# Batch 1's stage A moved onto quarter arrays: casting half loads of x, an earlier read of u, products from slot 8

## The chip, the cores and the metric

The kernel runs on one core of one Trainium2 chip. The metric is the device time of that core in microseconds (us), from the first instruction to the last. The time before is the median of three runs.

## The reference

```python
def _attn_ref(x, filt_r, filt_i):                 # x: 8 batches x 3008 rows x 256 channels
    X = np.fft.rfft(x, axis=1)
    Y = X * (filt_r + 1j * filt_i)[None, :, :]
    return np.fft.irfft(Y, n=x.shape[1], axis=1)

def _moe_ref(x, w_in, w_out):                     # 24064 rows, 256 -> 2048 -> 256
    h = np.maximum(x @ w_in, 0.0)
    return h * h @ w_out
```

The output is the second function of the first one's result: a filter by Fourier transform along the rows of each batch, then a feed-forward layer with a squared ReLU over all rows.

## The kernel before

A batch has 3008 = 64 x 47 rows, and its transform is done by matmuls in stages. Stage A takes x (64 blocks of 47) to **u**; u goes to DRAM (dU) and comes back in another order (`read_u`, tile ut). Stage B (`unit_b`) takes ut to frequencies and multiplies with the filter (DVE, the product), after which a DMA adds the two halves of the product. Stage P (`unit_p`) takes products to **z**; z goes to DRAM (dZ) and back (`read_z`, tile zt). Stage Y (`unit_y`) turns zt into yt, the input of the feed-forward layer.

The feed-forward layer runs in 47 groups of 512 rows, eight **slots** a group. Slot s does the first matmuls of group s // 8 (`ffn_g1`: four matmuls of 512 columns, then a ReLU on ACT into h, which DVE squares), and a share of the second matmuls of the group before (`ffn_g2` for the first group, `products` of seven half-size products with sums on DVE for the others). The stages of the later batches are put between these by a plan. Batch 0 goes through its stages ahead of slot 0, in a prologue.

Batch 1 is the special case that the change is about. Before, it loads x in float32 through SyncE's queue, casts it on three engines, and does stage A with full-array matmuls of 96 output rows, three quarters of it in the prologue and one quarter in slots 8 and 9:

```python
def load_wide(b, k):                              # 1 MB each, b = 0 and 1, k = 0..2
    ...
    nc.sync.dma_start(out=t, in_=(v0[:, 0:8, :], v1, v0[:, 8:16, :])[k])

def write_u(b, c):
    u = us.pop((b, c))
    if b == 1:
        nc.sync.dma_start(out=dU[b].rearrange("(m q) d -> q m d", q=96)[:, 8 * c:8 * c + 8, :], in_=u)
        return
    v = dU[b].rearrange("(m q) d -> q m d", q=48)
    for j in range(2):
        m = 16 * c + 8 * j
        nc.sync.dma_start(out=v[:, m:m + 8, :], in_=u[64 * j:64 * j + 48])

def unit_a1(b, a):                                # batch 1, one sixteenth; L354, L356
    ...
    nc.tensor.matmul(ps[0:96, :], s1[:, c // 2, :], xw16[(b, 2 * (c % 2))][:, m, :], start=True, stop=False)
    nc.tensor.matmul(ps[0:96, :], s1[0:120, 2 + c, :], xw16[(b, 1)][0:120, m, :], start=False, stop=True)
    ...                                           # copied to u by ACT (a even) or DVE (a odd)

def unit_a(b, c):                                 # batches 2 to 7, one quarter; L378
    u = us[(b, c)] = p_u.tile([112, 8, D], F16, tag="u", ...)
    ph = psH(...); ps = [psF(...) for h in range(2)]
    for i in range(2):
        for j in range(2):
            m = slice(4 * j + 2 * i, 4 * j + 2 * i + 2)
            for h in range(2):
                p = slice(64 * h, 64 * h + N2)
                o = ps[h] if i == 0 else ph[:, h, :]
                nc.tensor.matmul(o[64 * j:64 * j + 64, :], sSA[p], x16s[(b, c)][p, m, :], start=True, stop=True)
    ...                                           # three copies to u, then write_u

def chunk_a(b, c):                                # batch 1, one quarter, in the prologue; L400, L402
    ...                                           # 8 matmuls of 512 columns, copied to u by ACT or DVE

def load_x(b, k):                                 # half of a quarter of x, cast by the DMA
    ...
    nc.gpsimd.dma_start(out=t[64 * h + p0:64 * h + p1], in_=v[p0:p1, 8 * c:8 * c + 8, :])

def read_u(b):
    ut = p_ut.tile([128, NC, D], F16, tag="ut", name=f"ut_{b}")
    v = dU[b].rearrange("(p s) d -> p s d", s=NC)
    for s0, s1 in ((0, 8), (8, 24)):
        nc.sync.dma_start(out=ut[:, s0:s1, :], in_=v[:, s0:s1, :])
    uts[b] = ut
```

The end of the prologue and the plan's part for batch 1 (f is 0 there, and 40 for batch 2):

```python
cast_win()                                        # w_in to float16, GpSimd
for k in range(2):
    cast_wide(1, k, nc.gpsimd, nc.gpsimd)
...                                               # batch 0: stages B and P; each sixth of z is written to dZ
cast_wide(1, 2, nc.vector, nc.scalar)
read_z(0, 0)
load_wout(0)                                      # 1 MB
read_z(0, 1)
load_wout(1)                                      # 1 MB
for c in (0, 2, 1):
    chunk_a(1, c)
for c in (0, 2, 1):
    write_u(1, c)
for n in range(4):
    unit_y(0, n)
prologue[0] = False
read_z(0, 2)
...
    if b == 1:
        ...                                       # unit_y(0, n) for n = 4 to 15 in slots 4 to 23.5
        for a in range(12, 16):
            fixed.append((2 + a / 2, unit_a1, b, a))
        moves.append((10.5, read_u, b))
        d = 7
    ...
    for p in range(12):
        r = 14 + 15 * p / 11 if b == 1 else 6 + 28 * p / 11 if b == 2 else -2 + 36 * p / 11
        units.append((f + r, unit_b, b, p))
        if b == 1 and 2 <= p < 10:
            moves.append((f + r, load_x, 2, p - 2))
        units.append((f + r + (4.5 if b == 1 else 7 - 2.5 * p / 11), unit_p, b, p))
    for c in range(4):
        moves.append((f + (40 + d / 14, 43, 48, 54)[c] - d, read_z, b, c))
```

Engines run their instructions in program order, and so does SyncE's DMA queue: a transfer that waits holds up those behind it. [...]

Of the kernel before, what the change touches and what calls it, by code (L numbers as in the profile page):

```python
# [26 lines left out]
def _build_consts():  # L27
# [72 lines left out]
    f16 = lambda a, p: np.ascontiguousarray(a.reshape(p, -1).astype(np.float16))  # L100
    C0 = np.zeros((128, 1472))
    C0[:, 0:576] = S0.reshape(128, 6, 2, 2, NC).transpose(0, 1, 4, 2, 3).reshape(128, 576)
    C0[:, 576:704] = np.eye(128)
    C0[:, 704:1280] = S0.reshape(128, 576)
    for h in range(2):
        C0[64 * h:64 * h + N2, 1280:1328] = SA[:, h, h].reshape(N2, 48)
    C0[:, 1376:1470] = SY.reshape(128, 94)
    return f16(C0, 128), f16(PF, 128), f16(SB, 128), f16(SP, 128)


@with_exitstack
def kernel(
# [85 lines left out]

    sC0 = p_t.tile([128, 1280], F16, tag="t", name="sC0")
    sC1 = const.tile([128, 192], F16, name="sC1")  # L200
    nc.scalar.dma_start(out=sC0[:, 0:704], in_=dC0.ap()[:, 0:704])
    s0 = sC0[:, 0:576].rearrange("p (w q) -> p w q", q=96)
    s1 = sC0[:, 704:1280].rearrange("p (w q) -> p w q", q=96)
    sSA = sC1[:, 0:64]
    sSY = sC1[0:112, 96:190]
    ident = sC0[:, 576:704]
# [3 lines left out]

    def load_wide(b, k):

        v0 = xrows[b * S:b * S + 2048, :].rearrange("(p m) d -> p m d", m=16)
        v1 = xrows[b * S + 2048:b * S + 3072, :].rearrange("(p m) d -> p m d", m=8)
        pool, tag = (p_x32, "x32") if k < 2 else (p_y, "yt") if b else (p_h2, "h2")
        t = pool.tile([128, 8, D], F32, tag=tag, name=f"xw_{b}_{k}")
        nc.sync.dma_start(out=t, in_=(v0[:, 0:8, :], v1, v0[:, 8:16, :])[k])
        xw32[(b, k)] = t

    def cast(eng, out, in_):  # L220
        (eng.copy if eng is nc.scalar else eng.tensor_copy)(out=out, in_=in_)

    def cast_wide(b, k, *engs):
        t = p_x16.tile([128, 8, D], F16, tag="x16", name=f"xw16_{b}_{k}")
        for i in range(2):
            m = slice(4 * i, 4 * i + 4)
            cast(engs[i], t[:, m, :], xw32[(b, k)][:, m, :])
        xw16[(b, k)] = t

    for k in range(3):  # L230
        load_wide(0, k)

# [12 lines left out]
    load_f(1)  # L245
    nc.sync.dma_start(out=sC0[:, 704:1280], in_=dC0.ap()[:, 704:1280])
    nc.sync.dma_start(out=sC1, in_=dC0.ap()[:, 1280:1472])
    nyq = p_out.tile([128, 2, D], F32, tag="ost", name="nyq")
# [87 lines left out]
    def write_u(b, c):  # L336
        u = us.pop((b, c))
        if b == 1:
            nc.sync.dma_start(
                out=dU[b].rearrange("(m q) d -> q m d", q=96)[:, 8 * c:8 * c + 8, :], in_=u)  # L340
            return
        v = dU[b].rearrange("(m q) d -> q m d", q=48)
        for j in range(2):
            m = 16 * c + 8 * j
            nc.sync.dma_start(out=v[:, m:m + 8, :], in_=u[64 * j:64 * j + 48])

    def unit_a1(b, a):

        c, i = divmod(a, 4)
        if i == 0:  # L350
            us[(b, c)] = p_u.tile([96, 8, D], F16, tag="u", name=f"u_{b}_{c}")
        ps = psF(f"psA_{b}_{a}")
        m = slice(2 * i, 2 * i + 2)
        nc.tensor.matmul(ps[0:96, :], s1[:, c // 2, :], xw16[(b, 2 * (c % 2))][:, m, :],  # L354
                         start=True, stop=False)
        nc.tensor.matmul(ps[0:96, :], s1[0:120, 2 + c, :], xw16[(b, 1)][0:120, m, :],  # L356
                         start=False, stop=True)
        o = us[(b, c)][:, 2 * i:2 * i + 2, :]
        pv = ps[0:96, :].rearrange("p (a d) -> p a d", d=D)
        if a % 2 == 0:  # L360
            nc.scalar.copy(out=o, in_=pv)
        else:
            nc.vector.tensor_copy(out=o, in_=pv)
        if i == 3:
            write_u(b, c)

    def unit_a(b, c):

        u = us[(b, c)] = p_u.tile([112, 8, D], F16, tag="u", name=f"u_{b}_{c}")
        ph = psH(f"psA_{b}_{c}")  # L370
        ps = [psF(f"psA_{b}_{c}_{h}") for h in range(2)]
        for i in range(2):
            for j in range(2):
                m = slice(4 * j + 2 * i, 4 * j + 2 * i + 2)
# [3 lines that stand above are left out]
                    nc.tensor.matmul(o[64 * j:64 * j + 64, :], sSA[p], x16s[(b, c)][p, m, :],  # L378
                                     start=True, stop=True)
        for h in range(2):  # L380
            o = u[:, h:h + 3:2, :]
            pv = ps[h][0:112, :].rearrange("p (e d) -> p e d", d=D)
            if h == 0:
                nc.scalar.copy(out=o, in_=pv)
            else:
                nc.vector.tensor_copy(out=o, in_=pv)
        nc.scalar.copy(out=u[:, 4:8, :].rearrange("p (e h) d -> p h e d", h=2),
                       in_=ph[0:112].rearrange("p h (e d) -> p h e d", d=D))
        write_u(b, c)

    def chunk_a(b, c):

        u = p_u.tile([96, 8, D], F16, tag="u", name=f"u_{b}_{c}")
        us[(b, c)] = u
        for k in range(2):
            banks, groups = bank_pair(f"psA_{b}_{c}_{k}")
            for i in range(2):
                m = slice(4 * k + 2 * i, 4 * k + 2 * i + 2)
                o = banks[i][0:96]
                nc.tensor.matmul(o, s1[:, c // 2, :], xw16[(b, 2 * (c % 2))][:, m, :],  # L400
                                 start=True, stop=False)
                nc.tensor.matmul(o, s1[0:120, 2 + c, :], xw16[(b, 1)][0:120, m, :],  # L402
                                 start=False, stop=True)
            eng = pair_engine()
            for t, i in groups:
                n = t.shape[1]
                o = u[:, 4 * k + 2 * i:4 * k + 2 * i + 2 * n, :]
                pv = t[0:96].rearrange("p t (a d) -> p (t a) d", d=D)
                if eng is nc.scalar:
                    eng.copy(out=o, in_=pv)  # L410
                else:
                    eng.tensor_copy(out=o, in_=pv)

    def chunk_a0(c):

        for k in range(2):
            banks, groups = bank_pair(f"psA_0_{c}_{k}")
            for dt in range(2):
                for i in range(4):
                    m = 4 * k + i  # L420
                    o = banks[dt][:, 96 * i:96 * i + 96]
                    d = slice(128 * dt, 128 * dt + 128)
                    nc.tensor.matmul(o, xw16[(0, 2 * (c % 2))][:, m, d], s0[:, c // 2, :],
                                     start=True, stop=False)
                    nc.tensor.matmul(o, xw16[(0, 1)][0:120, m, d], s0[0:120, 2 + c, :],
                                     start=False, stop=True)
# [288 lines left out]
    def fft_plan():  # L715

        fixed, units, moves = [], [], []
        for b in range(1, B):
            f = (b * S // TG) * SLOTS - (48 if b > 1 else 40)
            d = 0  # L720
            if b == 1:
# [4 lines left out]
                for k in range(4):  # L726
                    moves.append(((4.5, 5.5, 7.5, 7.5)[k], cast_wout, k, nc.vector))
                for a in range(12, 16):
                    fixed.append((2 + a / 2, unit_a1, b, a))
                moves.append((10.5, read_u, b))  # L730
                d = 7
# [9 lines left out]
            for p in range(12):  # L741
                r = 14 + 15 * p / 11 if b == 1 else 6 + 28 * p / 11 if b == 2 else -2 + 36 * p / 11
                units.append((f + r, unit_b, b, p))
                if b == 1 and 2 <= p < 10:
                    moves.append((f + r, load_x, 2, p - 2))
                units.append((f + r + (4.5 if b == 1 else 7 - 2.5 * p / 11), unit_p, b, p))
# [38 lines left out]
    for k in range(3):  # L785
        cast_wide(0, k, nc.vector, nc.gpsimd if k == 2 else nc.vector)

# [8 lines left out]
    load_win()  # L796
    for k in range(3):
        load_wide(1, k)
    for c in (0, 2, 1, 3):
# [20 lines left out]
    for k in range(6):  # L820
# [3 lines left out]
        nc.gpsimd.tensor_copy(out=sSPx[-1][0:64, o, :], in_=sSP[64:128, c, :])  # L824
        nc.gpsimd.tensor_copy(out=sSPx[-1][64:128, o, :], in_=sSP[0:64, c, :])
    cast_win()
    for k in range(2):
        cast_wide(1, k, nc.gpsimd, nc.gpsimd)
    for k in range(7):
# [7 lines left out]
        if k < 4:  # L837
            place_f(0, k + 2, nc.scalar)
    cast_wide(1, 2, nc.vector, nc.scalar)
    read_z(0, 0)  # L840
    load_wout(0)
    read_z(0, 1)
    load_wout(1)
    for c in (0, 2, 1):
        chunk_a(1, c)
    for c in (0, 2, 1):
        write_u(1, c)
    for n in range(4):
# [55 lines left out]
```

## Time and profile before

| what | value |
|---|---|
| time, median of 3 (lowest to highest) | 760.14 us (759.89 to 760.58) |
| span of the profiled run | 758.9 us |
| TensorE busy in the records | 743.8 us, 98% |
| DVE, ACT, GpSimd busy | 653.1, 565.9, 191.7 us |
| prologue: first matmul of slot 0 | at 49.06 us |
| first matmul of slot 8 | at 58.24 us |
| casts of batch 1's x | GpSimd 34.94 to 38.9 us, DVE at 40.16, ACT at 41.84 |
| stage A of batch 1 in the prologue (24 matmuls) | 40.73 to 45.97 us |
| stage A of batch 1 in slots 8 and 9 (8 matmuls) | 59.61 to 63.96 us |
| `read_u` of batch 1, issue | at 68.17 us |
| first `unit_b` of batch 1, slot 14 | at 72.45 us |
| a GpSimd x load (batch 2 on), from issue to landing | 5.0 us median on the page |

The records of a matmul overlap[...]: one of 512 columns shows 380 ns, and the next can start 216 ns later. So a short wait is better seen between the starts of matmuls than in the idle time. A row of the stage table gives the stretch, its length, the busy time and number of instructions of each engine, then the granted clock, the share of the DMA engines and their rate. In the timeline of SyncE's queue the first number is the start and the second the time that the issues took with the waits among them.

### The profile page before, as it was taken

How to read it: one execution, taken by the hardware profiler on the slowest of the kernel's cores; microseconds unless marked ns; L12 is line 12 of the kernel's file. 1: busy time of each engine (PE TensorE's matmuls, PEld its weight loads, DVE VectorE, ACT ScalarE, POOL GpSimd, SP SyncE). 2: the span in 40 equal slices, each digit the busy share in tenths (PEclk: the TensorE clock that was granted, in tenths of full speed). 3: DMA queues.
4: the chain of work that ended last, by engine and by line, in shares of the span. 5: the costliest groups of instructions: out<-in, count | busy, mean ns of one | idle time of the engine just before them, and what ended most of it. 6: DMA issues, size and time to landing. Idle time of an engine off the chain costs nothing.

```text
span 758.9 us, 19877 instructions
## 1 busy us (share of the span) xinstructions
PE 743.8 (98%) x8358; PEld 544.3 (72%) x8358; DVE 653.1 (86%) x730; ACT 565.9 (75%) x801; POOL 191.7 (25%) x260
## 2 busy tenths in 40 slices
PE   8989998999999999999999999999999999999998
PEld 5846666776777777877778777787677777777776
DVE  5867997899899998999979998899988989888783
ACT  3976787777877777787777777777776777777773
POOL 3800750244222321233203224033311222000000
PEclk9999999999999999999999999999999999999999
DMA  9985797665776557755576646674547334321011
GB/s 366 393 233 187 131 191 206 176 124 114 161 206 138 95 127 187 172 105 131 108 211 137 127 102 129 201 153 101 114 111 191 90 72 98 98 85 44 30 57 56
DMA packets 103025, 109.26 MB, mean 144 GB/s; under 512 B 10016, under 2 KB 93472, under 8 KB 101016
## 3 DMA queue, kind: packets, MB, share of 16 engines
q1 hardware_dynamic: 86088, 87.38, 37.5%
q0 software_dynamic: 16704, 20.43, 19.4%
q8 instruction: 65, 1.06, 0.6%
q14 instruction: 24, 0.20, 0.1%
q10 hardware_dynamic: 144, 0.18, 0.1%
HBM read 58.12 MB, written 48.23 MB: 140 GB/s over the span
## 4 chain that ended last, share of the span: by engine, by line
PE 87%; DMA 5%; DVE 4%; ACT 2%; issue 1%; SPq 1%; POOL 0%; ACTq 0%; DVEq 0%; POOLq 0%
PE psH L576 38%; PE psX L689 19%; PE psY L689 15%; PE psY L546 3%; PE psB L465 2%; PE psP L510 2%; DMA zt<-dZ 2%; PE psO L596 2%; PE psA L378 2%; PE warm L268 1%; DMA dZ<-ze 1%; DVE prod L473 1%; DMA prod<-prod 1%; DMA dU<-u 1%; DVE h L587 1%
## 5 line engine op out<-in xcount | busy, mean ns | idle before, releaser
L580 ACT ACTIVATE h<-psH 128x1024 f16<-128x1024 f32 x376 | 385.4, 1026 | 162.2 <-PE psH L576 160.1
L576 PE MATMUL psH<-yt,sWin 128*128 128x512 f16 (+7 forms) x1728 | 387.0, 351 | 1.4 <-ACT h L580 0.5
L587 DVE TENSOR_TENSOR h<-h 128x2048 f16<-128x2048 f16 (+1 forms) x192 | 229.8, 1197 | 44.6 <-ACT h L580 44.3
L480 POOL DMA_DIRECT2D prod<-prod x168 | 139.3, 971 | 440.4 <-DVE prod L473 437.5
L576 PEld LDWEIGHTS <-sWin 128*128 128x128 f16 x1728 | 149.3, 98 | 91.1 <-issue 3.2
L689 PEld LDWEIGHTS <-sum 128*128 128x128 f16 x2880 | 177.4, 98 | 25.0 <-issue 5.6
L689 PEld LDWEIGHTS <-h 128*128 128x128 f16 x2160 | 132.6, 98 | 24.2 <-issue 5.3
L473 DVE TENSOR_TENSOR prod<-psB,sF 128x1024 f16<-128x1024 f32 x84 | 102.3, 1218 | 11.8 <-PE psB L465 11.7
L689 PE MATMUL psX<-sT,sum 128*128 128x128 f16 x1440 | 102.4, 219 | 0.0
L689 PE MATMUL psY<-sT,sum 128*128 128x128 f16 x720 | 69.7, 219 | 0.0
L665 DVE TENSOR_TENSOR sum<-sum,h 128x2048 f16<-128x2048 f16 x45 | 54.9, 1221 | 0.8
L689 PE MATMUL psY<-sWout,sum 128*128 128x128 f16 x720 | 54.8, 219 | 0.7 <-DVE bot L704 0.7
L689 PE MATMUL psY<-sWout,h 128*128 128x128 f16 x720 | 55.0, 219 | 0.0
L689 PE MATMUL psX<-sT,h 128*128 128x128 f16 x720 | 54.9, 219 | 0.0
L671 DVE TENSOR_TENSOR sum<-h,sum 128x2048 f16<-128x2048 f16 x45 | 54.7, 1216 | 0.0
L668 DVE TENSOR_TENSOR sum<-h 128x2048 f16<-128x2048 f16 x45 | 54.7, 1216 | 0.0
L662 DVE TENSOR_TENSOR sum<-h 128x2048 f16<-128x2048 f16 x45 | 54.7, 1216 | 0.0
L196 POOL DMA_DIRECT2D x<-in_x_dram x56 | 51.7, 1112 | 0.2 <-issue 0.2
L512 ACT CAST ze<-psP 128x512 f16<-128x512 f32 x84 | 49.2, 586 | 0.7 <-PE psP L510 0.4
L689 PE MATMUL psX<-sWout,h 128*128 128x128 f16 x720 | 47.6, 219 | 0.0
L546 PE MATMUL psY<-sC,zt 112*128 112x94 f16 x512 | 42.4, 205 | 4.2 <-DMA zt<-dZ 3.8
L555 DVE CAST yt<-psY 128x376 f16<-128x376 f32 x62 | 33.7, 543 | 14.5 <-PE psY L546 14.5
(87 smaller groups left out, 599.1 us busy)
## 6 DMA issues: line engine op xcount, KB each, us to landing
zt<-dZ SPq DMA_DIRECT2D x64, 192.0 KB
prod<-prod POOLq DMA_DIRECT2D x168, 64.0 KB, 2.7
dZ<-ze SPq DMA_DIRECT2D x28, 384.0 KB
dU<-u SPq DMA_DIRECT2D x48, 192.0 KB
x<-in_x_dram POOLq DMA_DIRECT2D x40, 192.0 KB, 5.0
ut<-dU SPq DMA_DIRECT2D x7, 1024.0 KB
xw<-in_x_dram SPq DMA_DIRECT2D x6, 1024.0 KB
out_dram<-top SPq DMA_DIRECT2D x31, 128.0 KB
```

The costliest lines, as they stand in the source:

```text
L196: nc.gpsimd.dma_start(out=t[64 * h + p0:64 * h + p1], in_=v[p0:p1, 8 * c:8 * c + 8, :])
L473: nc.vector.tensor_mul(out=prod, in0=ps.rearrange("p (a d) -> p a d", d=D).unsqueeze(1).to_broadcast([128, 2, 2, D]), in1=sF[:, :, 2 * p:2 ...
L480: nc.gpsimd.dma_start(out=prod[64 * i:64 * i + 64, 0], in_=prod[64 - 64 * i:128 - 64 * i, 1], accum_op=mybir.AluOpType.add)
L546: nc.tensor.matmul(ps[:, 94 * jj:94 * jj + 94], zt[:, 4 * (g % 2) + jj, dt * 128:(dt + 1) * 128], sSY, start=True, stop=True)
L576: nc.tensor.matmul(ps[:, i, o:o + n], sWin[:, dt, jt * 128:(jt + 1) * 128], yts[b][:, dt, r:r + n], start=(dt == 0), stop=(dt == 1))
L580: nc.scalar.activation(out=h2[:, 2 * s:2 * s + 2, :], in_=ps, func=AF.Relu)
L587: nc.vector.tensor_mul(out=v, in0=v, in1=v)
L662: nc.vector.tensor_add(out=t, in0=a21, in1=a22)
L665: nc.vector.tensor_sub(out=t, in0=f[5], in1=a11)
L668: nc.vector.tensor_sub(out=t, in0=a11, in1=a21)
L671: nc.vector.tensor_sub(out=t, in0=a12, in1=f[6])
L689: nc.tensor.matmul(o[:, t, :], f[p][:, q, 128 * t:128 * t + 128], sg["w"][p][:, q, :], start=(m == 0 and p in (1, 2)), stop=(q == 7), skip ...
```

## The change

Batch 1's x is no longer loaded wide in float32 and cast by GpSimd, DVE and ACT. It comes as eight half loads that GpSimd issues and the DMA casts, as for the later batches, two of them after each of the first four pairs of GpSimd's copies. Stage A of batch 1 becomes four `unit_a` on 64 x 64 quarters of the array, all in the prologue, where TensorE waits for batch 0's z to go to DRAM and back; the eight matmuls in slots 8 and 9 are gone, and so are `unit_a1`, `chunk_a` and their constants. u is written in eight transfers of 192 KB in place of four of 384 KB. `read_u` of batch 1 stands at slot 0 in place of 10.5, and its products are planned in slots 8 to 28 in place of 14 to 29. The aim is less work for TensorE, fewer casts, and products that are spread over more slots. The number of matmuls stays (8358).

```diff
-    def load_wide(b, k):
+    def load_wide(k):                              # batch 0 alone
 ...
     def write_u(b, c):
         u = us.pop((b, c))
-        if b == 1:
-            nc.sync.dma_start(
-                out=dU[b].rearrange("(m q) d -> q m d", q=96)[:, 8 * c:8 * c + 8, :], in_=u)
-            return
 ...
-    def unit_a1(b, a):
 ...
     def unit_a(b, c):
-        u = us[(b, c)] = p_u.tile([112, 8, D], F16, tag="u", name=f"u_{b}_{c}")
+        pool, tag = (p_y, "yt") if (b, c) == (1, 3) else (p_u, "u")
+        u = us[(b, c)] = pool.tile([112, 8, D], F16, tag=tag, name=f"u_{b}_{c}")
         ph = psH(f"psA_{b}_{c}")
-        ps = [psF(f"psA_{b}_{c}_{h}") for h in range(2)]
+        if b == 1 and c % 2:
+            ps = [psO(...) for h in range(2)]
+        else:
+            ps = [psF(f"psA_{b}_{c}_{h}") for h in range(2)]
 ...                                               # batch 1: ACT copies both ps, DVE copies ph
-    def chunk_a(b, c):
 ...
-                for a in range(12, 16):
-                    fixed.append((2 + a / 2, unit_a1, b, a))
-                moves.append((10.5, read_u, b))
+                moves.append((0, read_u, b))
 ...
-                r = 14 + 15 * p / 11 if b == 1 else ...
+                r = 8 + 20 * p / 11 if b == 1 else ...
 ...
-    for k in range(3):
-        load_wide(1, k)
 ...
         nc.gpsimd.tensor_copy(out=sSPx[-1][64:128, o, :], in_=sSP[0:64, c, :])
+        if k < 4:
+            load_x(1, 2 * k)
+            load_x(1, 2 * k + 1)
     cast_win()
-    for k in range(2):
-        cast_wide(1, k, nc.gpsimd, nc.gpsimd)
 ...
-    cast_wide(1, 2, nc.vector, nc.scalar)
     read_z(0, 0)
     load_wout(0)
     read_z(0, 1)
     load_wout(1)
-    for c in (0, 2, 1):
-        chunk_a(1, c)
-    for c in (0, 2, 1):
-        write_u(1, c)
+    for c in range(4):
+        unit_a(1, c)
     for n in range(4):
         unit_y(0, n)
     prologue[0] = False
     read_z(0, 2)
```

More of the change, by code (lines that the diff above doesn't have):

```diff
@@ L100, in _build_consts @@
     f16 = lambda a, p: np.ascontiguousarray(a.reshape(p, -1).astype(np.float16))
-    C0 = np.zeros((128, 1472))
+    C0 = np.zeros((128, 896))
     C0[:, 0:576] = S0.reshape(128, 6, 2, 2, NC).transpose(0, 1, 4, 2, 3).reshape(128, 576)
     C0[:, 576:704] = np.eye(128)
-    C0[:, 704:1280] = S0.reshape(128, 576)
     for h in range(2):
-        C0[64 * h:64 * h + N2, 1280:1328] = SA[:, h, h].reshape(N2, 48)
-    C0[:, 1376:1470] = SY.reshape(128, 94)
+        C0[64 * h:64 * h + N2, 704:752] = SA[:, h, h].reshape(N2, 48)
+    C0[:, 768:862] = SY.reshape(128, 94)
     return f16(C0, 128), f16(PF, 128), f16(SB, 128), f16(SP, 128)
@@ L197, in load_x @@
                                 in_=v[p0:p1, 8 * c:8 * c + 8, :])
-    sC0 = p_t.tile([128, 1280], F16, tag="t", name="sC0")
+    sC0 = p_t.tile([128, 704], F16, tag="t", name="sC0")
     sC1 = const.tile([128, 192], F16, name="sC1")
-    nc.scalar.dma_start(out=sC0[:, 0:704], in_=dC0.ap()[:, 0:704])
+    nc.scalar.dma_start(out=sC0, in_=dC0.ap()[:, 0:704])
     s0 = sC0[:, 0:576].rearrange("p (w q) -> p w q", q=96)
-    s1 = sC0[:, 704:1280].rearrange("p (w q) -> p w q", q=96)
     sSA = sC1[:, 0:64]
-    sSY = sC1[0:112, 96:190]
+    sSY = sC1[0:112, 64:158]
     ident = sC0[:, 576:704]
@@ L209, with cast_wide @@
     xw32, xw16 = {}, {}
-    def load_wide(b, k):
[L213 to L216, printed above, removed]
+    def load_wide(k):
+        v0 = xrows[0:2048, :].rearrange("(p m) d -> p m d", m=16)
+        v1 = xrows[2048:3072, :].rearrange("(p m) d -> p m d", m=8)
+        pool, tag = (p_x32, "x32") if k < 2 else (p_h2, "h2")
+        t = pool.tile([128, 8, D], F32, tag=tag, name=f"xw_{k}")
         nc.sync.dma_start(out=t, in_=(v0[:, 0:8, :], v1, v0[:, 8:16, :])[k])
-        xw32[(b, k)] = t
+        xw32[k] = t
     def cast(eng, out, in_):
         (eng.copy if eng is nc.scalar else eng.tensor_copy)(out=out, in_=in_)
-    def cast_wide(b, k, *engs):
-        t = p_x16.tile([128, 8, D], F16, tag="x16", name=f"xw16_{b}_{k}")
+    def cast_wide(k, *engs):
+        t = p_x16.tile([128, 8, D], F16, tag="x16", name=f"xw16_{k}")
         for i in range(2):
             m = slice(4 * i, 4 * i + 4)
-            cast(engs[i], t[:, m, :], xw32[(b, k)][:, m, :])
-        xw16[(b, k)] = t
+            cast(engs[i], t[:, m, :], xw32[k][:, m, :])
+        xw16[k] = t
     for k in range(3):
-        load_wide(0, k)
+        load_wide(k)
     f32s = []
@@ L245 @@
     load_f(1)
-    nc.sync.dma_start(out=sC0[:, 704:1280], in_=dC0.ap()[:, 704:1280])
-    nc.sync.dma_start(out=sC1, in_=dC0.ap()[:, 1280:1472])
+    nc.sync.dma_start(out=sC1, in_=dC0.ap()[:, 704:896])
     nyq = p_out.tile([128, 2, D], F32, tag="ost", name="nyq")
@@ L345, in write_u, with unit_a @@
             nc.sync.dma_start(out=v[:, m:m + 8, :], in_=u[64 * j:64 * j + 48])
-    def unit_a1(b, a):
[L349 to L361, printed above, removed]
-        else:
[L363 to L367, printed above, removed]
-        u = us[(b, c)] = p_u.tile([112, 8, D], F16, tag="u", name=f"u_{b}_{c}")
-        ph = psH(f"psA_{b}_{c}")
-        ps = [psF(f"psA_{b}_{c}_{h}") for h in range(2)]
+    def unit_a(b, c):
+        pool, tag = (p_y, "yt") if (b, c) == (1, 3) else (p_u, "u")
+        u = us[(b, c)] = pool.tile([112, 8, D], F16, tag=tag, name=f"u_{b}_{c}")
+        ph = psH(f"psA_{b}_{c}")
+        if b == 1 and c % 2:
+            ps = [psO(f"psA_{b}_{c}_{h}").rearrange("p a d -> p (a d)") for h in range(2)]
+        else:
+            ps = [psF(f"psA_{b}_{c}_{h}") for h in range(2)]
         for i in range(2):
@@ L382, in unit_a @@
             pv = ps[h][0:112, :].rearrange("p (e d) -> p e d", d=D)
-            if h == 0:
+            if h == 0 or b == 1:
                 nc.scalar.copy(out=o, in_=pv)
@@ L386, in unit_a @@
                 nc.vector.tensor_copy(out=o, in_=pv)
-        nc.scalar.copy(out=u[:, 4:8, :].rearrange("p (e h) d -> p h e d", h=2),
-                       in_=ph[0:112].rearrange("p h (e d) -> p h e d", d=D))
-        write_u(b, c)
-    def chunk_a(b, c):
-        u = p_u.tile([96, 8, D], F16, tag="u", name=f"u_{b}_{c}")
-        us[(b, c)] = u
-        for k in range(2):
[L396 to L412, printed above, removed]
+        o = u[:, 4:8, :].rearrange("p (e h) d -> p h e d", h=2)
+        pv = ph[0:112].rearrange("p h (e d) -> p h e d", d=D)
+        if b == 1:
+            nc.vector.tensor_copy(out=o, in_=pv)
+        else:
+            nc.scalar.copy(out=o, in_=pv)
+        write_u(b, c)
     def chunk_a0(c):
@@ L422, in chunk_a0 @@
                     d = slice(128 * dt, 128 * dt + 128)
-                    nc.tensor.matmul(o, xw16[(0, 2 * (c % 2))][:, m, d], s0[:, c // 2, :],
+                    nc.tensor.matmul(o, xw16[2 * (c % 2)][:, m, d], s0[:, c // 2, :],
                                      start=True, stop=False)
-                    nc.tensor.matmul(o, xw16[(0, 1)][0:120, m, d], s0[0:120, 2 + c, :],
+                    nc.tensor.matmul(o, xw16[1][0:120, m, d], s0[0:120, 2 + c, :],
                                      start=False, stop=True)
@@ L741, in fft_plan @@
             for p in range(12):
-                r = 14 + 15 * p / 11 if b == 1 else 6 + 28 * p / 11 if b == 2 else -2 + 36 * p / 11
+                r = 8 + 20 * p / 11 if b == 1 else 6 + 28 * p / 11 if b == 2 else -2 + 36 * p / 11
                 units.append((f + r, unit_b, b, p))
@@ L785 @@
     for k in range(3):
-        cast_wide(0, k, nc.vector, nc.gpsimd if k == 2 else nc.vector)
+        cast_wide(k, nc.vector, nc.gpsimd if k == 2 else nc.vector)
     def load_const(t, d, k):
@@ L825 @@
         nc.gpsimd.tensor_copy(out=sSPx[-1][64:128, o, :], in_=sSP[0:64, c, :])
+        if k < 4:
+            load_x(1, 2 * k)
+            load_x(1, 2 * k + 1)
     cast_win()
-    for k in range(2):
-        cast_wide(1, k, nc.gpsimd, nc.gpsimd)
     for k in range(7):
```

## The prediction

> **What bounds the kernel now.** I read the page's engine shares and its chain first, then the table of stages over the first 160 us (the change touches nothing after slot 40), then TensorE's waits, and last the timelines of TensorE and of SyncE's queue at the places where TensorE stands.
>
> ```profile
> PE 743.8 (98%) x8358; PEld 544.3 (72%) x8358; DVE 653.1 (86%) x730; ACT 565.9 (75%) x801; POOL 191.7 (25%) x260
> PE 87%; DMA 5%; DVE 4%; ACT 2%; issue 1%; SPq 1%; POOL 0%; ACTq 0%; DVEq 0%; POOLq 0%
> ```
>
> TensorE sets the time: 87% of the chain is its own work. The rest is a few waits, and these lie early:
>
> ```profile
> 44.00:48.00 4.00, 2.79 (x21) 1.60 (x20) 1.68 (x2) 2.07 (x3) 0.00 (x0) 1.00 0.67 199
> 56.00:60.00 4.00, 3.47 (x22) 1.66 (x20) 4.00 (x7) 3.12 (x4) 0.00 (x0) 1.00 1.08 335
> 60.00:64.00 4.00, 4.00 (x28) 2.69 (x27) 1.93 (x3) 2.99 (x4) 0.00 (x0) 1.00 0.26 72
> 80.00:84.00 4.00, 3.53 (x40) 2.52 (x38) 4.00 (x4) 2.68 (x4) 1.26 (x3) 1.00 0.58 83
> 96.00:100.00 4.00, 3.63 (x31) 2.01 (x29) 3.97 (x4) 2.94 (x6) 2.07 (x3) 1.00 1.02 205
> 120.00:124.00 4.00, 2.87 (x32) 1.46 (x30) 2.42 (x3) 3.63 (x6) 0.00 (x0) 1.00 0.69 191
> PE psY L546 <- DMA zt<-dZ: 2.9, 2, 1.9
> ```
>
> Four stages, four limits. At 44 to 48 TensorE waits for batch 0's z. From 49 to 60 (slots 0 to 7) ACT and DVE pace it, and the DMA engines are full (share 1.08). From 60 to 76 TensorE is the bound without a gap. From 76 to 108 DVE is full (4.00 of 4.00), and TensorE loses a little. At 120 to 124 it waits 1.9 us for batch 1's z.
>
> ```profile
> 45.75 0.38 PE L402 MATMUL psA<-xw,sC 120*96 120x512 f16 x1
> 46.41 0.27 PE L544 MATMUL psY<-zero 128*128 128x128 f16 x2 [0.29 <-ACT u L410]
> 47.61 0.33 PE L546 MATMUL psY<-sC,zt 112*128 112x94 f16 x4 [0.93 <-DMA zt<-dZ]
> ...
> 59.61 0.38 PE L354 MATMUL psA<-xw,sC 128*96 128x512 f16 x1
> 59.82 0.38 PE L356 MATMUL psA<-xw,sC 120*96 120x512 f16 x1
> 60.04 1.04 PE L596 MATMUL psO<-sWout,h 128*128 128x256 f16 x8
> ```
>
> The prologue's stage A ends inside the wait for z, so making it shorter gains nothing there. A pair of stage A in slots 8 and 9 costs 0.43 us (59.61 to 60.04) and nothing hides it.
>
> ```profile
> 47.32 7.11 SPq L339 DMA_DIRECT2D dU<-u  x3
> 54.52 4.76 SPq L528 DMA_DIRECT2D zt<-dZ  x4
> ...
> 64.91 0.32 SPq L339 DMA_DIRECT2D dU<-u  x1
> 68.17 0.82 SPq L456 DMA_DIRECT2D ut<-dU  x2
> ```
>
> Three writes of u take SyncE's queue seven microseconds to hand over, because two megabytes of w_out stand ahead of them. The read of u comes long after, at 68.17, four microseconds ahead of its use.
>
> [...] the eight matmuls of a `unit_a` (L378) start at 108.75 and what follows starts at 109.31, so 0.56 us, not 8 x 0.216 = 1.73[...]. [...] an 8 KB float32 packet of the wide load shows 0.309 us, a casting packet that reads the same 8 KB shows 0.324. [...] The trace shows both paces at the start, 427 ns between warm-up matmuls until 8.1 us and 216 after[...].
>
> **The change, part by part.**
>
> 1. *Loads and casts.* GpSimd loses four casts (34.94 to 38.9) and gains eight issues; pairs of such issues take 1.0 to 1.65 us later on, say 1.3, so 5.2 us. Its copies for stage P end at 30.5 + 5.2 = 35.8 and are wanted by 39.17; the casts of w_in end at 40.2 and are wanted at 49.06. The last load is issued at about 33 and lands 5 us later, ahead of 40.7. DVE and ACT lose one cast each (0.68 and 1.05 us) that stood after their part of batch 0's chain. The same 3 MB is read. Worth: 0.
>
> 2. *Stage A in the prologue.* 24 matmuls of 0.218 us (5.24 us) become 4 x 0.56 = 2.2 us plus waits for the copies. batch 0's last ze is done at 41.95, its write lands at 44.31, zt at 47.48, and nothing in these is changed. TensorE just waits longer. Slot 0 stays at 49.06. Worth: 0.
>
> 3. *Slots 8 and 9.* 4 x 0.43 = 1.73 us leave a stretch that TensorE bounds. Worth: **-1.7**.
>
> 4. *The read of u against slot 8.* The first product of batch 1 now stands in slot 8, where TensorE would be at 59.6. By the packets in the trace (1,024 B are w_out, 512 B are u, 4,096 B the reads), the second megabyte of w_out is through at 54.5, then three u writes take until 58.2, some 320 KB per us. A fourth (384 KB) makes it 59.3. The read has to wait for all eight to land, some 0.5 us more, so it is issued at 59.8. Before, its first half megabyte was through 3.3 us after its issue (68.17 to 71.4). So ut is there at 63.1, and TensorE, which runs in order, stands from 59.6 to 63.1. Worth: **+3.5**.
>
> 5. *Products earlier.* Five are done ahead of slot 16 in place of two, so three (3 x 1.13 = 3.4 us) leave DVE's full stretch. From starts of matmuls against their pace, TensorE loses 0.65, 0.24, 0.36, 0.40 and 0.77 us in slots 19 to 27, 2.4 in sum. In slots 16 to 23 DVE would still have four squares (4.5), four sums (4.7), four products (4.5), and small ones (some 2.2): 15.9 us against 16.2 of matmuls. Nearly full, so I take 0.9 as left. Worth: **-1.5**.
>
> 6. *Batch 1's z.* The chain of waits there reads: write of batch 2's u 111.30 to 118.47, write of z to 121.71, read of z to 124.66. The write of z was ready at 114.4 but stood in SyncE's queue behind that u write, which four casting x loads (issued 107.85 to 110.7) had slowed. With the products a slot earlier, two of these four go out sooner, since GpSimd gets to them after the last product. I expect the u write some 2 us sooner, and most of the 2.1 us between starts gone. Worth: **-1.5**.
>
> 7. *Clock.* [...] One chance in four: **+0.4**.
>
> Sum: -1.7 + 3.5 - 1.5 - 1.5 + 0.4 = -0.8, so 760.14 - 0.8 = **759.3 us**.
>
> **The rivals.** *No new wait*: if u gets out ahead of w_out's second half, or the read of u needs less than 3.3 us, part 4 falls away, and the time is 760.1 - 4.7 = 755.4. For it: the u tiles are ready some microseconds before 47.3. Against it: one queue in order, and DMA engines that are full until 60. *A longer wait*: eight smaller writes need more issues[...]; if the last one is issued only at w_out's landing plus two microseconds, the read slips to 61 and the sum to +0.5 or more. *Nothing comes back later*: DVE stays full and z still stands behind u's write; then -1.7 + 3.5 = +1.8, 762. *A clock drop in the prologue*, where TensorE is idle from about 45 to 47.6: its cost would be swallowed by part 4, since the read of u does not depend on TensorE.
>
> **Range and chances.** The parts that could fail are 4 (0 to 4.5), 5 and 6 (0 to 2 each), and they partly offset: a late read delays slots and gives z more time. 756.3 to 762.0 holds most of this. Two per cent is 15 us, four times the largest part, so same has 0.98.
>
> **What would show it.** Slot 0 at 49 us in both. In slot 8 a wait of the first `unit_b` for ut of about 3.5 us, with the read of u issued near 59.8. No L354. Slots 9 to 15 without gaps. DVE below full between 64 and 108, and TensorE's loss in slots 19 to 27 under 1 us. The wait for zt in slot 38 under 1 us. Wrong if slot 0 moves by over 1 us, if `unit_b` does not wait in slot 8, or if slots after 40 take another time than before.

## The result, and the profile after

The changed kernel takes **764.55 us** (median of four, 763.72 to 765.42) against 760.01 beside it; the ratio is 1.006, with an interval of 1.0042 to 1.0077. So it is slower by some 4.5 us, within two per cent, and above the predicted range, which ended at 762.0.

The shares of the engines and the chain, from the page of the kernel after:

```profile
PE 741.7 (97%) x8358; PEld 542.3 (71%) x8358; DVE 653.3 (86%) x727; ACT 564.5 (74%) x801; POOL 191.6 (25%) x264
PE 87%; DMA 6%; DVE 3%; ACT 2%; SPq 1%; issue 1%; POOL 0%; DVEq 0%; ACTq 0%
```

TensorE has two microseconds less in the records, and DMA one per cent more of the chain. TensorE's waits from 20 to 140 us (total, times, longest) and its timeline say where:

```profile
PE psB L423 <- DMA ut<-dU: 4.1, 1, 4.1
PE psY L504 <- DMA zt<-dZ: 3.2, 2, 2.8
...
42.13 2.57 PE L355 MATMUL psA<-x,sC 47*64 47x512 f16 x20 [0.33 <-ACT ze L456]
...
47.72 0.47 PE L504 MATMUL psY<-sC,zt 112*128 112x94 f16 x4 [2.79 <-DMA zt<-dZ]
...
49.80 2.60 PE L534 MATMUL psH<-yt,sWin 128*128 128x512 f16 x8
...
65.15 0.61 PE L423 MATMUL psB<-ut,sSB 128*128 128x256 f16 x2 [4.08 <-DMA ut<-dU]
65.56 1.91 PE L554 MATMUL psO<-sWout,h 128*128 128x256 f16 x8
```

Two things are to be seen. Slot 8 waits for u, as predicted, but longer. And after each of the two waits the matmuls are slow: eight of 256 columns show 1.91 us, where the kernel before shows 1.04. The stage table has the reason in its granted clock, the third number from the end:

```profile
47.00:48.00 1.00, 0.28 (x5) 0.32 (x6) 0.00 (x0) 0.00 (x0) 0.00 (x0) 0.84 1.06 305
48.00:51.00 3.00, 2.95 (x24) 1.99 (x22) 1.10 (x2) 0.94 (x2) 0.00 (x0) 0.50 1.10 313
51.00:52.00 1.00, 1.00 (x5) 0.39 (x4) 0.00 (x0) 0.37 (x1) 0.00 (x0) 0.95 0.99 182
64.00:65.00 1.00, 0.00 (x0) 0.00 (x0) 0.00 (x0) 0.00 (x0) 0.00 (x0) 0.87 1.04 434
65.00:68.00 3.00, 2.85 (x12) 1.80 (x13) 1.23 (x1) 0.00 (x0) 0.67 (x2) 0.50 1.04 355
68.00:69.00 1.00, 1.00 (x7) 0.61 (x6) 0.00 (x0) 0.22 (x1) 1.00 (x2) 0.92 0.56 91
```

Worked out from the shares in the first and last row of each group, TensorE ran at half its clock from 47.68 to 51.10 and from 64.75 to 68.16, 3.41 us each. In the kernel before the clock stays full from 8 us to the end of this execution.

SyncE's queue after, between 46 and 62 us:

```profile
46.97 10.49 SPq L338 DMA_DIRECT2D dU<-u  x8
57.57 1.38 SPq L486 DMA_DIRECT2D zt<-dZ  x2
61.29 0.82 SPq L414 DMA_DIRECT2D ut<-dU  x2
```

Eight writes of u take 10.5 us to hand over, and the read of u is issued at 61.29. By the starts of slots, the changed kernel is behind the one before by 1.3 us at slot 8, 5.7 at slot 10, 4.5 at slot 31 and 2.8 at slot 40; the spans differ by 2.7 (761.6 and 758.9). The profiled execution is the quickest of the four, with a mean granted clock of 0.995; the others have 0.991 to 0.993. A stretch of 3.41 us at half the clock takes 0.0022 off this mean (3.41 x 0.5 / 762). So 0.995 stands for the two stretches of the trace, and the others had, by this estimate, three to four. Where these lay is not on record.

### The profile page after: what moved, and what is told of

Same layout as the page of the kernel before. It is cut to its first block, busy times and chain, and to the rows that moved or that the text cites. A ratio compares the mean times of both kernels' runs of the same rounds, so it can differ in the third digit from the quotient of the medians.

```text
span 761.6 us, 19875 instructions
## 1 busy us (share of the span) xinstructions
PE 741.7 (97%) x8358; PEld 542.3 (71%) x8358; DVE 653.3 (86%) x727; ACT 564.5 (74%) x801; POOL 191.6 (25%) x264
## 4 chain that ended last, share of the span: by engine, by line
PE 87%; DMA 6%; DVE 3%; ACT 2%; SPq 1%; issue 1%; POOL 0%; DVEq 0%; ACTq 0%
PE psH L534 39%; PE psX L647 20%; PE psY L647 15%; PE psY L504 3%; PE psB L423 2%; PE psP L468 2%; DMA f<-in_filt_i_dram 2%; PE psO L554 2%; PE psA L355 2%; DVE prod L431 1%; SPq L338 1%; DMA zt<-dZ 1%; DMA prod<-prod 1%; DMA dZ<-ze 1%; DVE h L545 1%
## 5 line engine op out<-in xcount | busy, mean ns | idle before, releaser
L545 DVE TENSOR_TENSOR h<-h 128x2048 f16<-128x2048 f16 (+1 forms) x192 | 229.9, 1198 | 46.8 <-ACT h L538 46.4
L195 POOL DMA_DIRECT2D x<-in_x_dram x64 | 55.3, 1030 | 2.2 <-PE psA L355 2.2
```

The costliest lines, as they stand in the source:

```text
L545: nc.vector.tensor_mul(out=v, in0=v, in1=v)
```

## The experiments

My theory after the result: u goes out and back behind two megabytes of w_out in one queue, and the idle array loses its clock at both waits. The rivals: the casting loads or the quarter-array stage A cost the time; or the eight writes of u do by themselves; or the slow clock costs nothing. Each run was timed beside the kernel before, which took 760.25, 760.07 and 759.91 us in the three groups of runs.

**1. The schedule undone, the rest kept.**

```diff
-                moves.append((0, read_u, b))
+                moves.append((10.5, read_u, b))
-                r = 8 + 20 * p / 11 if b == 1 else ...
+                r = 14 + 15 * p / 11 if b == 1 else ...
```

> The changed kernel with the read of u back at slot 10.5 and the products back in slots 14 to 29; loads and stage A stay as changed. Theory (the early read meets u writes that stand behind w_out, and the idle array then loses its clock): no wait for ut in slot 8, no slow clock from 64 us on; slots 0 and 1 still start late, by 1.3 us at slot 2, since batch 0's z is waited for with an idle array; the eight matmuls of slots 8 and 9 are gone (-1.7). So 759 to 760.5 us. DVE's gaps in slots 19 to 27 come back (about 2 us). Rival (the casting loads or the quarter-array stage A themselves cost the time): stays at 763 or over.

Measured: 760.43 us, ratio 0.9996 (0.9984 to 1.0008). The loads and the new stage A are not what costs the 4.5 us: with the late read the kernel is level with the one before. But it is level, not 1.7 us faster. Its stage table tells why:

```profile
43.00:44.00 1.00, 0.81 (x8) 0.24 (x8) 1.00 (x2) 1.00 (x4) 0.00 (x0) 0.89 0.49 151
44.00:54.00 10.00, 7.71 (x47) 3.66 (x41) 3.90 (x5) 4.40 (x8) 0.00 (x0) 0.50 0.95 254
54.00:55.00 1.00, 0.93 (x4) 0.29 (x3) 0.00 (x0) 0.97 (x2) 0.00 (x0) 0.99 1.09 348
```

Half the clock for ten microseconds, and it fell at 43.8, while quarter-array matmuls were still running. (This execution is the slowest of the twelve, with a mean clock of 0.993; most of the others have 0.995.)

**2. One megabyte of w_out behind the u writes.**

```diff
     read_z(0, 1)
-    load_wout(1)
     for c in range(4):
         unit_a(1, c)
+    load_wout(1)
```

> The changed kernel with one line moved: the second megabyte of w_out is loaded after batch 1's u writes in place of before them. Theory: the u writes are through some 3 us sooner, the read of u is issued at about 57 to 58 in place of 61.3, the wait for ut in slot 8 falls from 4.1 to under 1 us, and the clock does not fall there; the first fall, in slots 0 to 2, stays. 758 to 760.5 us, unless the casts of w_out's second half now hold slot 9. Rival (the wait is the sheer number of issues and their turns, not w_out): the read of u stays after 60 and the time at 763 or over.

Measured: 766.05 us, 1.0067 (1.0046 to 1.0088); no better. From SyncE's queue and TensorE's timeline:

```profile
46.72 7.68 SPq L338 DMA_DIRECT2D dU<-u  x8
54.44 0.90 SPq L325 DMA_DIRECT2D wout<-in_moe_w_out_dram  x1
...
57.47 0.91 SPq L414 DMA_DIRECT2D ut<-dU  x2
...
64.44 0.61 PE L423 MATMUL psB<-ut,sSB 128*128 128x256 f16 x2 [2.01 <-DMA ut<-dU]
```

The step about the writes held: the read is issued at 57.47, 3.8 us sooner. But the read then takes seven microseconds, since the megabyte now stands between it and the writes, and u is used at 64.44 in place of 65.15. What counted was all that the queue carried ahead of the read's last byte. The wait fell from 4.1 to 2.0 mostly because TensorE came later: the clock fell at 47.3 and stayed low for 6.8 us. In slot 8 the clock fell all the same, at 64.4, after a wait of only 2.0 us. That the time did not come down is a miss of my expectation.

**3 and 4. Fillers in the waits.** Matmuls on zeros, overwritten by what follows; run 3 has the first part, run 4 both.

```diff
+        if prologue[0] and n == 0:                 # ahead of batch 0's first stage Y
+            for _ in range(12):
+                nc.tensor.matmul(ps, zero, sF[:, 0, 0:2, :], start=True, stop=True)
 ...
+        if b == 1 and p == 0:                      # ahead of batch 1's first stage B
+            for _ in range(18):
+                nc.tensor.matmul(ps, zero, sF[:, 0, 0:2, :], start=True, stop=True)
```

> The changed kernel with twelve matmuls of 512 columns on zeros put ahead of batch 0's first stage Y matmul, into a bank that is overwritten right after; they fill 2.6 us of the wait for z. Theory: the clock stays full, slot 0 starts at about 49.1 and slot 2 at 51.4 as in the kernel before, 1.3 us sooner; but the read of u does not depend on TensorE, so the wait in slot 8 grows by as much and the time stays within 1 us of the changed kernel's 763.7 to 765.4. Rival (each loss adds): 1.3 us less, 762.4 to 764.

> As the run before, with eighteen more such matmuls ahead of batch 1's first stage B matmul, which fill 3.9 us of the wait for ut. Theory: the clock stays full after that wait too, so some 1.3 to 2.5 us less than the changed kernel: 762 to 763, and runs that lie within 0.5 us of each other, where the changed kernel's fall into two groups at 763.8 and 765.3. Rival (the matmuls after the wait are slow for another reason, as full DMA engines): no change.

Run 3: 765.18 us, 1.0063 (1.0043 to 1.0082), level with the changed kernel; four executions. Run 4: 762.28 us, 1.0025 (1.0017 to 1.0033), sixteen executions between 761.8 and 763.5. TensorE's timeline in run 3, then in run 4:

```profile
48.83 2.03 PE L537 MATMUL psH<-yt,sWin 128*128 128x512 f16 x8 [0.28 <-ACT yt L514]
...
64.39 0.61 PE L423 MATMUL psB<-ut,sSB 128*128 128x256 f16 x2 [4.86 <-DMA ut<-dU]
```

```profile
59.84 4.05 PE L424 MATMUL psB<-sF,zero 128*128 128x512 f16 x18
64.91 0.38 PE L426 MATMUL psB<-ut,sSB 128*128 128x256 f16 x2 [1.02 <-DMA ut<-dU]
65.12 1.03 PE L560 MATMUL psO<-sWout,h 128*128 128x256 f16 x8
```

In run 3 slot 0 starts at 48.83 in place of 49.80, and slot 8 just waits longer, 4.9 us: the first loss is swallowed by the second wait. In run 4 the first stage B still starts at 64.91, since u decides that, but the second layer then runs at full pace (1.03, not 1.91). The full DMA engines are not the reason for the slow matmuls, since run 4 leaves the transfers as they are: from 64 to 66 us the DMA share is 1.07 there and 1.05 in the changed kernel, the granted clock 1.00 and 0.69. Against the changed kernel run 4 is 2.3 us quicker, as expected.

What one fall costs is read from the traces: from the first stage B to slot 11 run 3 takes 6.24 us (64.39 to 70.63), run 4 takes 4.95 (64.91 to 69.86), so 1.3 us. The medians of the two runs differ by more, 2.9. That is a difference over executions and not the price of one fall: the two traced executions took the same time (762.26 and 762.27 us), and run 3's is the quickest of its four. The other three have a mean clock of 0.995 or 0.996 where the traced one has 0.998, so about one slow stretch more; run 4's executions have 0.998 to 1.0.

**5, 6 and 8. w_out out of the way.** Run 5 loads all of w_out behind w_in, into batch 1's free buffers; run 6 adds the twelve fillers; run 8 loads one half there, the other behind the read of u, with the fillers.

```diff
     load_win()
+    load_wout(0)
+    load_wout(1)                                   # run 8: behind read_u(1)
 ...
     read_z(0, 0)
-    load_wout(0)
     read_z(0, 1)
-    load_wout(1)
```

> The changed kernel with both megabytes of w_out loaded right behind w_in, long before batch 0's z, into the two buffers that batch 1's float32 x has left free. Theory (u's way out and back stands behind w_out in the DMA rings): the read of u is issued near 53 and lands by 57 to 58, no wait in slot 8 and no slow clock after it; the slow clock in slots 0 and 1 stays and is no longer swallowed. 756.5 to 758.5 us, if the fuller DMA engines do not delay batch 0's z. Rival (the wait for u is the time of its own eight writes and the read): the wait in slot 8 stays over 2 us and the time over 761. Rival (z is delayed by w_out): slot 0 starts at 51 or later, 759 to 760.

> As the run before, with the twelve matmuls on zeros in the wait for z. Theory: the clock stays full throughout, 1.3 to 2 us less than the run before: 755 to 757 us, below both the kernel before and the changed one. Rival (the slow clock in slots 0 to 3 costs nothing, since ACT paces them): the same time as the run before.

> As the run with w_out early and the twelve matmuls, but the second megabyte of w_out is loaded behind the read of u. Theory: u gets out and back as soon as with both early, batch 0's z is not delayed by the second megabyte, but its casts come at about 61 to 62, close to the second matmuls that need them in slot 9. 755 to 757.5 us. Rival (z is not delayed by w_out at all): no better than with both early.

Measured: run 5 764.04 us, 1.0044 (1.0028 to 1.006); run 6 763.25, 1.0044 (1.0032 to 1.0057); run 8 768.97, 1.0116 (1.0089 to 1.0144). All three missed. Run 5's chain and wait:

```profile
25.27 19.42 DMA wout<-in_moe_w_out_dram
44.69 4.57 DMA dZ<-ze
...
PE psY L503 <- DMA zt<-dZ: 8.0, 1, 8.0
...
50.75 6.78 SPq L337 DMA_DIRECT2D dU<-u  x8
...
60.42 0.82 SPq L413 DMA_DIRECT2D ut<-dU  x2
```

Batch 0's z now stands behind w_out, and slot 0 starts at 55.0. This was my second rival for run 5, but far larger than I had put it. u's writes stand behind z in turn, so the read of u is issued at 60.42, hardly sooner than the 61.29 of the changed kernel; that slot 8 no longer waits is due to its later start, 65.00 and not 59.54.

How much of u's way out is w_out can still be read. From the handing over of the first write to the issue of the read it takes 14.3 us in the changed kernel (46.97 to 61.29), 10.8 in run 2 with one megabyte of w_out ahead, and 9.7 in run 5 with none (10.3 in run 8). So w_out is some 4 to 5 us of it; the larger part, about 10 us, is the eight writes themselves and what runs beside them. Whether fewer and larger writes would be through sooner no run shows.

From slot 8 to slot 40 run 5 needs 64.8 us (65.00 to 129.81), the kernel before 69.4 (58.24 to 127.67). These 4.6 us are close to what the prediction's parts 3, 5 and 6 promise together (4.7) once nothing waits for u.

In run 6 twelve matmuls could not bridge an eight-microsecond wait: the clock stayed low for 6.8 us from 51.1 on, so that run does not tell whether a slow clock there costs anything. In run 8 one megabyte ahead of z is enough to bring zt 1.9 us later (49.62, not 47.72), and the half behind the read of u comes too late for slot 9:

```profile
PE psO L558 <- DVE sWout L329: 6.3, 1, 6.3
```

**7. Late read, with the fillers.** Run 1's edit and run 3's together.

> The changed kernel with the read of u at slot 10.5, the products in slots 14 to 29, and the twelve matmuls on zeros in the wait for z. The same with no such matmuls took 760.4. Theory (what the removed matmuls of slots 8 and 9 gained was lost to the clock in slots 0 to 3): the loss is won back, 757.8 to 759 us. Rival (the clock there costs nothing): 760.4.

Measured: 758.58 us, 0.9973 (0.9963 to 0.9984), twenty executions. It is some 1.8 us below run 1, which differs in the twelve fillers alone. So the slow clock ahead of slot 4 does cost time once nothing swallows it. The fillers do not always keep it away: in the traced execution, one of the slowest of the twenty (759.63 us, mean clock 0.997), it fell at 43.4, ahead of the fillers and in the midst of the quarter-array stage A, and was back at 46.8:

```profile
43.00:44.00 1.00, 0.89 (x9) 0.27 (x8) 1.00 (x1) 1.00 (x3) 0.00 (x0) 0.70 0.80 234
```

The other nineteen have 0.999 or 1.0.

**9. The read at slot 0, products from slot 11.5, with the fillers.**

```diff
-                r = 8 + 20 * p / 11 if b == 1 else ...
+                r = 11.5 + 17 * p / 11 if b == 1 else ...
```

> The changed kernel with the read of u at slot 0, the products in slots 11.5 to 28.5, and the twelve matmuls on zeros in the wait for z. Theory (the read of u lands at 65.1 whatever TensorE does, and slot 11 reaches its first stage B matmul at about 66): no wait for ut, full clock, and part of what the early products gained in slots 19 to 27 and 38 is kept. 756.5 to 758.5 us, up to 1.5 us below the run with products from slot 14 (758.6). Rival (the products' place does not matter once nothing waits for u): the same 758.6.

Measured: **757.53 us**, 0.9959 (0.9944 to 0.9974): 2.4 us below the kernel before in the medians, 7 below the changed one. TensorE in slot 11 waits for nothing, and the clock is full:

```profile
64.48 1.03 PE L537 MATMUL psH<-yt,sWin 128*128 128x512 f16 x4
65.49 0.38 PE L423 MATMUL psB<-ut,sSB 128*128 128x256 f16 x2
65.71 1.03 PE L557 MATMUL psO<-sWout,h 128*128 128x256 f16 x8
...
60.00:76.00 16.00, 16.00 (x125) 11.09 (x124) 13.13 (x15) 10.55 (x14) 4.48 (x7) 1.00 0.64 183
```

That it is below run 7 is likely, but not shown: their intervals overlap, and they were not timed side by side.

**10. The kernel before with fillers.** Five of them, in its wait for z.

> The kernel before with five such matmuls on zeros in its wait for z (0.9 us of it is empty). Theory: its clock is full there in nearly all runs, so nothing is won: 759.5 to 760.3 us. Rival (the filling itself is what makes the filled kernels faster, whatever the stage A): 758.6 us.

Measured: 759.25 us, 0.9987 (0.9977 to 0.9997). Beside it the kernel before had 6 of 21 executions at 760.6 to 763.4 with a mean clock of 0.996 or 0.998; with the fillers, 16 executions lie between 758.6 and 760.7 at 0.999 or 1.0. So that kernel loses its clock now and then too, which I had not expected, and some 0.7 us of what runs 7 and 9 gain is this. Filling alone does not give 758.6.

## Why the prediction was wrong, point by point

- **Parts 1 and 3** held. The loads land in time and no copy for stage P comes late. Slots 8 and 9 of run 7 take 3.98 us, of run 10 5.72: 1.74 less, as put.
- **Part 2** did not hold: slot 0 starts at 49.80 and not at 49.06, and slot 8 1.3 us late. Stage A, 32 quarter-array matmuls, is over at 44.7, z comes at 47.72, and the clock has just fallen. This is my rival of a clock drop in the prologue, and part 4's wait swallowed it, as I had put (run 3).
- **Part 4** had the right mechanism and was too small: +3.5 was put. The second layer of slot 8 starts at 65.56 where the kernel before has it at 60.04, so **+5.5**. The failed terms are the read's issue, 61.29 and not 59.8, and its time, 3.9 us and not 3.3. My rival of a longer wait had put the read's issue at 61. By the packets, the eight writes end near 60.5, not 59.3: the read of batch 0's third zt, issued at 57.57, shares their last microsecond. I had put it behind them.
- **Part 5**: the gaps of slots 16 to 27 (the short ones where stage A begins or ends not counted) are 1.4 us after, 2.4 before. So -1.0, not -1.5. I had expected DVE to have room; in these slots it is busy for 23.8 of 24.5 us, before 26.0 of 26.2, so it is still nearly full, and a stage A that waits for a product costs 0.7 us of what is left.
- **Part 6** held. The recorded wait for batch 1's z is 0.4 us, not 1.9; between starts 0.55, not 2.10. Two of the four x loads go out at 110.3, ahead of the u write, which delays the write of z by 5.6 us, not 7.2.
- **Part 7** is the step that failed, beside the size of part 4. I gave the clock one chance in four to fall at slot 8 and put +0.4 for it, so some 1.6 us for one fall. Chance and price were my estimates. The price was about right: TensorE works at half pace from 65.15 to 68.16, so 1.5 us are lost (1.3 in run 3). The chance was not: the clock fell in slot 8 in all three profiles in which a wait there was left unfilled (changed kernel, runs 2 and 3). Nor was the count: I allowed for one fall, and the slower executions have, by their mean clocks, three to four slow stretches. I also took the kernel before to keep its full clock after the start, as its trace does; six of its 21 executions beside run 10, with a mean clock of 0.996 or 0.998, did not.

For the traced execution the sum is -1.7 + 5.5 - 1.0 - 1.5 + 1.5 = +2.8, and it is 2.8 us behind at slot 40 and 2.7 at the end. The medians differ by 4.5. The 1.7 between fit one slow stretch more in the usual execution, but no trace shows that one. The range was too narrow since I took the clock for a small addend instead of a second outcome.

## What to carry to other kernels

A read placed earlier in the program need not be much earlier on the chip: at slot 0 the read of u was issued at 61.29 us, at slot 10.5 at 62.04 (run 1). Add up the bytes ahead of it, the writes it depends on and what runs beside it, and put the consumer where that sum ends (run 9), or nothing is won. When TensorE's work inside a wait is made smaller, ask what the idle array does to the clock; a dozen matmuls on zeros in that wait gave back some 1.8 us here (run 7 against run 1). Moving the obstacle up the same queue can just hand the wait to the next transfer in it, as run 5 did with z (a wait of 8.0 us).

## What the runs showed of the hardware that I had not expected

The half clock comes in stretches of a few lengths. Those between 40 and 80 us last 3.41 us twice in the changed kernel, about as long in runs 3 and 7, 6.8 and 3.4 us in run 2, 6.8 in run 6, and 10.2 in runs 1 and 5, read from the clock of their stage tables: about one, two or three times 3.41. The two falls of the changed kernel lie 17.07 us apart, which is five times. The executions of one kernel differ in their mean clocks, 0.991 to 0.995 for the changed one. What decides how many slow stretches a wait costs is not shown, since a trace exists of one execution each.

One fall came in 2.79 us of recorded idle time, in the changed kernel, another in 2.0 us, in run 2. Nor was TensorE idle for the whole 3.41 us ahead of them: it was busy for 0.65 us from 44.27 to 47.68 in the changed kernel, and for 0.94 us from 60.99 to 64.40 in run 2. In the kernel before, 45.56 to 48.98 with 2.01 us was followed by no fall.

With quarter-array matmuls at work the clock fell once and stayed full once at nearly the same busy time: from 40 to 44 us TensorE was busy for 2.97 us in run 7, where it fell at 43.4, and for 3.01 us in the changed kernel, where it stayed full until 47.68. Why, no run shows, since none varied stage A by itself.
